# Products of half chunks dealt evenly to four array parts, one bank fewer per gate, masks first, and v's load first, in a one-core kernel of linear attention and a gated FFN

## The chip, the core and the metric

The kernel runs on one core of one Trainium2 chip. Its engines work side by side: TensorE (PE, matmuls; its weight loads are shown as PEld), VectorE (DVE), ScalarE (ACT), GpSimd (POOL) and SyncE (SP, which here only starts transfers). PE writes into PSUM, eight banks of 128 partitions by 2 KB, which DVE and ACT read; everything else lies in SBUF. The metric is the time of one execution in microseconds (us), as the median of several runs.

## The reference

The first half is gated linear attention for 4 batches of 8 heads, 768 steps, 48 values a head; the second is a multiplicative feed-forward network over the 3072 rows that this gives:

```
for t in range(S):                              # per batch b and head h
    state = alpha[t][:, None] * state + outer(k[t], v[t])     # 48 x 48
    y[t]  = q[t] @ state
x = y as 3072 rows of 384 (8 heads x 48)
out = (((x @ w1) * (x @ w2)) @ w3) @ w_out      # 384 -> 1024 -> 1024 -> 384
```

q, k, v and alpha are float32; the four weights come as float64.

## The kernel before

**Attention by chunks.** The 768 steps of a batch are cut into six chunks of C = 128, so there are N = 24 chunks, and the loop over n (L729 to L829) takes one chunk per step with all eight heads at once. For a chunk, `logs` and `decays` make the running products e of alpha (and their inverses) from a sum of logarithms; `decayed` (L357) multiplies q and k by them on DVE into qk; `transposed` turns qk on PE, 64 rows at a time, into qkT, whose two copies out of PSUM ACT makes (L383). `scores` forms all products of k and q in a chunk, and DVE clears what lies in the future with the masks of L440 and L457, which gives ms ("masks" below). A chunk's output y is then the sum of two products in PSUM: `attend_state` (L463), the state T of before the chunk times q, and `attend` (L477), v times ms. `outer` (L393) makes the next state from k and v, and at some chunks `advance` (L405) multiplies it on POOL with decays that have come back from DRAM. At each step n the order is: state and y's first part of chunk n-1, scores of chunk n, transposes of chunk n+1, `advance` and `turn_v`, the rest of y of chunk n-1, outer product of chunk n; in between, pieces of other work are dealt out (below).

**The array's parts.** Heads are worked on in pairs: the head pair j (0 to 3) has its two heads (i = 0, 1) in the partitions 0 to 47 and 64 to 111. A matmul that contracts over at most 64 partitions and writes at most 64 partitions occupies one of four parts of PE's array, given by the half of the rows that it reads from (i) and the half of the partitions that it writes; matmuls on different parts run at the same time. From chunk TURNED = 8 on, `turned_scores` (L422) leaves out the scores that the masks would clear: a chunk is cut into two halves of 64 steps, and the scores of the later half's keys are made for the later half's queries only. So of each head the part that takes the earlier keys streams 128 columns, the other 64. What is left out of the masks saves attention work as well: queries of the earlier half need v's earlier half only, and this product is `attend_low` (L415). It contracts over 64 steps, and for the second head of a pair over v with its halves exchanged, which `turn_v` (L162) makes by two copies on POOL into `vts`. `attend_low` of chunk n-1 is woven into the scores of chunk n, two matmuls behind each j:

```
if turned(n - 1):
    for i in range(2):
        attend_low(n - 1, j % 2, i, i ^ (j < 2))
```

The last argument is the half of the partitions that it writes: with j = 0 and 1 the part is (i, 1-i), with j = 2 and 3 it is (i, i). The longer scores of head i fall on part (i, i). After the last chunk, L755 to L757 issue these lows without scores.

**Where y lies.** y of a chunk has two banks, one for each row half i; in a bank, pair j lies in the upper or lower partitions and its 128 queries side by side. `attend_state` writes each with one matmul of 128 columns (8 for a chunk), the two kinds of v products add to it, and two copies on ACT (L489) bring it to SBUF, from where `store` sends it to the DRAM array xd.

**The gates and the rest.** A float32 product is made of parts rounded for PE: x and w are split in three (high, low, and a third that both corrections share), and `products` (L554) runs K/128 matmuls each for two of the parts into one group, and K/128 for the third. `exact` (L557) does this with two banks: ACT copies the first, scaled, to SBUF (L563), and DVE scales the second and adds it (L565). `onto` (L575) uses one bank: ACT scales it in place (L579), and the third part's matmuls are put off in a list `pending` until `settle` runs them on top. A gate tile is one 128-row piece of (x @ w1) * (x @ w2) for the columns of a group of three or four chunks; early gates, those made while attention runs, use `exact` for both factors, and DVE multiplies them (L602):

```
for factor, scale in zip(factors(g, f), (1.0, P * P)):
    r.append(gw.tile([C, width], FP32, tag="g", name="r"))
    exact(r[-1], *factor, scale)
```

Early gates wait in the list `fill`; `run(pieces)` takes one half tile (one factor, nine matmuls) per piece, at three places of a step, so that there are up to three in a step. The groups are begun by `begin` (L723): group g at chunk 3+4g, with `split_early` splitting its x at the step that is two later. Late gates use `onto` for both factors; behind attention they run with the folding of w3 @ w_out into one matrix w3o (`fold`), and then `project` multiplies chunk by chunk with it.

**The start.** Until step FIRST = 6 there are no gates; the steps then convert w1 and w2 from float64 (`convert`, pieces of `to_fp32`, L244 to L253) on ACT and DVE, beside the attention of the first chunks. `load_early(0)` reads x of the first three chunks back (L512).

**What sets the order.** Each engine runs its instructions in the order in which the program issues them, unless `after_marks` holds one back behind a marked instruction of another engine's list; a scheduler may set instructions that are held back behind later ones. In the loop of before, `decayed(n + 2)` is held behind the masks of chunk n only for n < 3. SyncE's queue takes loads and stores in the program's order: `store` (y), `load_a` (alpha), `load_kq`, then `load_v` (L154), which for chunks 3 to 7 goes by POOL's queue. The pool of PSUM has eight banks, dealt out in turn: a new bank is the one that was freed first, and the first matmul into it waits until it is read.

Of the kernel before, what the change touches and what calls it, by code (L numbers as in the profile page):

```python
# [10 lines left out]
FP32 = mybir.dt.float32  # L11
# [9 lines left out]
P = 4096.0  # L21
# [27 lines left out]
def kernel(  # L49
# [112 lines left out]
    def turn_v(n):  # L162
        if turned(n):
            for half in range(2):
                nc.gpsimd.tensor_copy(out=vts[n % 2][ds(DP * half, DP), :, 0:D],
                                      in_=st["v", n][ds(DP * (1 - half), DP), 1::2, 0:D])
# [248 lines left out]
    def attend_low(n, jj, i, half):  # L415

        s, w = ds(DP * i, DP), (vts[n % 2] if i else st["v", n])
        h = half * NP // 2 + jj
        nc.tensor.matmul(st["y", n][0][i][ds(DP * half, DP), jj, 0:DP], w[s, h if i else 2 * h, :],  # L419
                         st["ms", n][s, i, h, 0:DP], start=(n % NCH == 0 and jj == 0), stop=True, skip_group_check=True)  # L420

    def turned_scores(n):  # L422
# [3 lines left out]
        for j in range(NP):  # L426
# [5 lines left out]
            if turned(n - 1):  # L432
                for i in range(2):
                    attend_low(n - 1, j % 2, i, i ^ (j < 2))
# [30 lines left out]

# [11 lines left out]
    def attend(n):  # L477
        (y, heads), ms, vc = st.pop(("y", n)), st.pop(("ms", n)), st.pop(("v", n))
        for j, i, to in heads:
            if turned(n):  # L480
                w = vts[n % 2][:, j, :] if i else vc[:, 2 * j, :]
                nc.tensor.matmul(to[:, DP:], w, ms[:, i, j, DP:], start=False,  # L482
                                 stop=(j % HP == HP - 1), skip_group_check=True)
            else:
                nc.tensor.matmul(to, vc[:, 2 * j + i, :], ms[:, i, j, :], start=(n % NCH == 0 and j % HP == 0),  # L485
                                 stop=(j % HP == HP - 1), skip_group_check=True)
        x = work.tile([C, HP, 2, C], FP32, tag="x", name="x", bufs=4)
        for i in range(2):
            copied = nc.scalar.copy(x[:, :, i], y[i])  # L489
        ends_of_part1[1] = copied.ins  # L490
        x = x.rearrange("p j i t -> p (j i) t")

        to = xd.rearrange("(b h d) t -> b d h t", b=2, d=D)
# [63 lines left out]
    def exact(to, w, x, scale, in_place=True):  # L557
# [5 lines left out]
        nc.scalar.activation(t, p1, AF.Copy, scale=(1.0 + 1.0 / P) * scale)  # L563
        products(p2, w, x, (2,), n, True, True)
# [357 lines left out]
```

## Time and profile before

| | |
|---|---|
| median of 3 runs | 463.27 us (463.22 to 464.31) |
| the profiled execution | 462.59 us |
| its span, first to last instruction | 460.9 us |
| PE busy | 446.0 us (97%), 4080 matmuls |
| DVE busy | 370.6 us (80%) |
| ACT busy | 270.7 us (59%) |
| POOL busy | 87.4 us (19%) |
| granted TensorE clock | 0.999 |

The span falls into three stretches, whose busy times are:

| stretch, us | what runs | PE | DVE | ACT |
|---|---|---|---|---|
| 0 to 57 | start: loads, conversion of w1 and w2, chunks 0 to 6 | 47.95 | 41.70 | 39.48 |
| 57 to 187 | attention, chunks 6 to 23, with early gates | 127.78 | 117.81 | 82.20 |
| 187 to 457 | late gates, w3 @ w_out, projection | 270.00 | 210.53 | 149.05 |

A busy time is the time in which at least one instruction of the engine ran, in an execution recorded by the hardware profiler. Matmuls overlap, and their ends are modelled, so what a group of them costs is read from one first start to the next group's first start. "bank" is the name of every PSUM tile, and "L554" the line of the kernel that issued an instruction.

### The profile page before, as it was taken

To read this page: it belongs to the slowest core of one execution; us is meant where nothing else is said; L and a number is where in the kernel's file an instruction comes from. 1 tells how busy PE (TensorE), PEld (TensorE's weight loads), DVE (VectorE), ACT (ScalarE), POOL (GpSimd) and SP (SyncE) were. 2 spreads that over 40 slices of the span, in tenths; PEclk is the share of its full clock that TensorE was granted. 3 is DMA by queue.
4 is the path that set the end of the run, shared out by engine and by line. 5 is a ranking of instruction groups with operands and counts; after the bars stand their busy time and mean duration, and the time that the engine had idled before them with its cause. 6 is when DMAs were issued, how large, how long until landed. Compare 5 with 4: busy or idle time off the path is not lost.

```text
span 460.9 us, 10654 instructions
## 1 busy us (share of the span) xinstructions
PE 446.0 (97%) x4080; PEld 394.6 (86%) x4080; DVE 370.6 (80%) x600; ACT 270.7 (59%) x507; POOL 87.4 (19%) x171
## 2 busy tenths in 40 slices
PE   4998999899999999999999999999999999999996
PEld 2676699898989988888888888888888999999996
DVE  2897997999979989798999899999537566776671
ACT  4685966667668563787975757566436333343430
POOL 6134332324414370012021010100000000000000
PEclk9999999999999999999999999999999999999999
DMA  9999999989999965436966364521119655665511
GB/s 174 258 215 226 263 216 208 233 208 226 188 225 186 254 153 167 138 102 187 302 193 207 118 172 133 175 70 46 48 51 288 197 151 165 188 186 158 160 53 51
DMA packets 149379, 79.95 MB, mean 173 GB/s; under 512 B 97184, under 2 KB 138784, under 8 KB 149328
## 3 DMA queue, kind: packets, MB, share of 16 engines
q1 hardware_dynamic: 143840, 64.84, 57.0%
q0 software_dynamic: 5488, 14.43, 10.5%
q8 instruction: 32, 0.52, 0.5%
q14 instruction: 19, 0.16, 0.1%
HBM read 57.19 MB, written 22.06 MB: 172 GB/s over the span
## 4 chain that ended last, share of the span: by engine, by line
PE 89%; DVE 6%; issue 2%; ACT 2%; DMA 1%; DVEq 0%; ACTq 0%
PE bank L554 73%; PE bank L381 3%; PE bank L430 3%; PE bank L482 2%; PE bank L474 2%; DVE qk L359 1%; PE bank L393 1%; PE bank L340 1%; PE bank L346 1%; DVE ms L457 1%; PE bank L454 1%; PE bank L343 1%; PE bank L419 1%; PE bank L485 1%; DMA ac<-in_alpha_dram 1%
## 5 line engine op out<-in xcount | busy, mean ns | idle before, releaser
L554 PE MATMUL bank<-x,w 128*128 128x512 f32 (+1 forms) x688 | 162.7, 374 | 1.5 <-ACT qkT L383 1.2
L554 PEld LDWEIGHTS bank<-x,w 128*128 128x128 f32 x688 | 124.8, 188 | 21.3 <-ACT qkT L383 1.5
L554 PE MATMUL bank<-w3o,ab 128*128 128x384 f32 x576 | 100.2, 336 | 0.0
L554 PEld LDWEIGHTS bank<-w3o,ab 128*128 128x128 f32 x576 | 99.9, 188 | 0.2
L554 PE MATMUL bank<-x3b,w 128*128 128x512 f32 (+1 forms) x248 | 71.9, 385 | 0.0
L579 ACT ACTIVATE bank<-bank 128x512 f32<-128x512 f32 (+1 forms) x72 | 41.0, 571 | 33.1 <-PE bank L554 33.1
L554 PEld LDWEIGHTS bank<-x3b,w 128*128 128x128 f32 x248 | 46.4, 188 | 8.3
L628 POOL DMA_DIRECT2D abd<-r x33 | 19.3, 584 | 138.1 <-DVE r L614 116.2
L678 DVE TENSOR_TENSOR ab<-abl,ab 128x1024 fp32r<-128x1024 f32 x24 | 29.4, 1224 | 14.2 <-ACT ab L677 14.2
L383 ACT COPY qkT<-bank 128x512 f32<-128x512 f32 x48 | 26.1, 599 | 23.1 <-PE bank L381 23.1
L563 ACT ACTIVATE t<-bank 128x384 f32<-128x384 f32 x24 | 11.8, 493 | 45.9 <-PE bank L554 45.9
L677 ACT ACTIVATE ab<-abl 128x1024 fp32r<-128x1024 f32 x24 | 25.5, 1062 | 21.8 <-PE bank L554 19.8
L554 PE MATMUL bank<-wo,w3T 128*128 128x384 f32 x192 | 36.3, 337 | 0.0
L554 PEld LDWEIGHTS bank<-wo,w3T 128*128 128x128 f32 x192 | 34.1, 188 | 1.2
L565 DVE SCALAR_TENSOR_TENSOR o<-bank,t 128x384 f32<-128x384 f32 x24 | 13.4, 558 | 26.1 <-issue 14.3
L249 ACT ACTIVATE power<-power,rebias 128x512 uint32<-128x512 uint32 (+1 forms) x36 | 25.2, 701 | 15.0 <-DVE power L248 14.7
L359 DVE TENSOR_TENSOR qk<-kq,e 128x768 f32<-128x768 f32 x24 | 23.2, 965 | 10.5 <-ACT e L350 7.7
L565 DVE SCALAR_TENSOR_TENSOR r<-bank,r 128x384 f32<-128x384 f32 (+1 forms) x40 | 22.9, 578 | 8.5 <-ACT r L563 5.0
L563 ACT ACTIVATE r<-bank 128x384 f32<-128x384 f32 (+1 forms) x40 | 20.8, 524 | 14.7 <-PE bank L554 12.5
L614 DVE TENSOR_TENSOR r<-bank,r 128x512 f32<-128x512 f32 x32 | 21.9, 684 | 9.2 <-PE bank L554 7.7
L679 DVE SCALAR_TENSOR_TENSOR ab<-ab,abl 128x1024 fp32r<-128x1024 f32 x24 | 29.2, 1218 | 0.0
L251 DVE SCALAR_TENSOR_TENSOR mant<-mant,raw 128x512 f32<-128x512 uint32 (+1 forms) x36 | 23.5, 652 | 2.6 <-ACT raw L244 2.6
(115 smaller groups left out, 741.7 us busy)
## 6 DMA issues: line engine op xcount, KB each, us to landing
abl<-abd SPq DMA_DIRECT2D x24, 512.0 KB, 4.2
abd<-r POOLq DMA_DIRECT2D x33, 256.0 KB, 3.5
raw<-in_moe_w_dram SPq DMA_DIRECT2D x64, 128.0 KB, 3.7
raw<-in_moe_w_dram SPq DMA_DIRECT2D x12, 512.0 KB, 5.9
kq<-in_k_dram SPq DMA_DIRECT2D x24, 192.0 KB, 5.0
kq<-in_q_dram SPq DMA_DIRECT2D x24, 192.0 KB, 5.4
xd<-x SPq DMA_DIRECT2D x48, 96.0 KB, 3.7
xT<-xd POOLq DMA_DIRECT2D x6, 768.0 KB, 5.3
```

The lines of the kernel that those rows point to most:

```text
L249: nc.scalar.activation(power, power, AF.Relu, scale=2.0 ** 23, bias=rebias)
L251: nc.vector.scalar_tensor_tensor(mant, top, 2.0 ** -20, rest, op0=ALU.mult, op1=ALU.add)
L359: mark["qk", n] = nc.vector.tensor_mul(qks[n % 3][:, :, :, 0:D], st.pop(("kq", n)), st.pop(("e", n)).rearrange("p i (h d) -> p i h d", h=H ...
L383: mark["qkT", n] = nc.scalar.copy(qkT[:, :, :, ds(DP * half, DP)], tp[half]).ins
L554: nc.tensor.matmul(p, w[part][i], x[part][i], start=start and part == parts[0] and i == 0, stop=stop and part == parts[-1] and i == n - 1, ...
L563: nc.scalar.activation(t, p1, AF.Copy, scale=(1.0 + 1.0 / P) * scale)
L565: nc.vector.scalar_tensor_tensor(to, p2, scale, t, op0=ALU.mult, op1=ALU.add)
L579: nc.scalar.activation(p, p, AF.Copy, scale=1.0 + 1.0 / P)
L614: nc.vector.tensor_mul(r[0], p, r[0])
L677: nc.scalar.activation(t[:, 0], ab, AF.Copy, scale=1.0 - 2.0 ** -13)
L678: nc.vector.tensor_sub(t[:, 1], ab, t[:, 0].bitcast(FP32))
L679: nc.vector.scalar_tensor_tensor(t[:, 2], t[:, 0].bitcast(FP32), -1.0 - 1.0 / P, ab, op0=ALU.mult, op1=ALU.add)
```

## The change

It has five parts.

1. **Products dealt evenly.** y of a turned chunk is laid out anew: one bank holds the queries of the later half of a chunk, y[0], the other those of the earlier half, y[1], for all four pairs j. `attend_low` now always writes the half 1-i of the partitions, so that all lows fall on the parts (0, 1) and (1, 0), which take the shorter scores. `attend_state` cuts each product with the state into two of 64 columns, one for each half of the queries, and deals them to all four parts: 16 matmuls of 64 columns in place of 8 of 128. Both row halves i now write into one bank, in opposite halves of its partitions; before, each bank had one row half only. `attend` copies y[1] first, by two copies of 64 partitions each, because its heads lie exchanged, then makes the later half's products into y[0] and copies it whole. y is stored by head instead of by half of the heads.
2. **The second factor of an early gate** is made by `onto`: ACT scales the bank in place, the last three matmuls of nine are put off, and DVE multiplies the bank with the first factor directly. `exact` gets a hook `between`, where the pending matmuls of the tile before are run, behind the first six matmuls of the next first factor; a `settle()` behind `outer` runs them too. The last tile of a group (`begin_last`) keeps `exact` for both factors. The scale P * P goes to the first factor.
3. **Masks first.** `decayed(n + 2)` is held behind the masks of chunk n for n <= 6 instead of n < 3.
4. **v's load first.** From step 6 on `load_v(n + 2)` stands first in the step, ahead of stores and of the loads of alpha, k and q; before step 6 it stands behind `advance` instead of ahead of the conversion.
5. **v's turning earlier.** `turn_v(n + 1)` runs near the end of step n, where `turn_v(n)` ran in step n; `advance(n)` is held behind it.

```
-    def attend_low(n, jj, i, half):
-        s, w = ds(DP * i, DP), (vts[n % 2] if i else st["v", n])
-        h = half * NP // 2 + jj
-        nc.tensor.matmul(st["y", n][0][i][ds(DP * half, DP), jj, 0:DP], w[s, h if i else 2 * h, :],
-                         st["ms", n][s, i, h, 0:DP], start=(n % NCH == 0 and jj == 0), stop=True, skip_group_check=True)
+    def attend_low(n, j, i):
+        s, w = ds(DP * i, DP), (vts[n % 2][:, j, :] if i else st["v", n][:, 2 * j, :])
+        nc.tensor.matmul(st["y", n][1][ds(DP * (1 - i), DP), j, :], w[s], st["ms", n][s, i, j, 0:DP],
+                         start=(n % NCH == 0 and j == 0), stop=(j == NP - 1), skip_group_check=True)
...
     def attend_state(n):
         qkT = st.pop(("qkT", n))
+        if turned(n):
+            y = st["y", n] = [bank()[:, 0:NP * DP].rearrange("p (j c) -> p j c", c=DP) for _ in range(2)]
+            if n % NCH:
+                for j in range(NP):
+                    for t in range(2):
+                        for i in range(2):
+                            r = ds(DP * i, D)
+                            nc.tensor.matmul(y[t][ds(DP * (i ^ t), DP), j, :], Ts[n % 2][r, j, :],
+                                             qkT[r, 1, j, ds(DP * (1 - t), DP)],
+                                             start=(j == 0), stop=False, skip_group_check=True)
+            return
...
     def attend(n):
...
+        if turned(n):
+            x = work.tile([C, NP, C], FP32, tag="x", name="x", bufs=4)
+            for i in range(2):
+                nc.scalar.copy(x[ds(DP * i, DP), :, 0:DP], y[1][ds(DP * (1 - i), DP)])
+            for j in range(NP):
+                for i in range(2):
+                    nc.tensor.matmul(y[0][ds(DP * i, DP), j, :], vts[n % 2][:, j, :] if i else vc[:, 2 * j, :], ms[:, i, j, DP:],
+                                     start=(n % NCH == 0 and j == 0), stop=(j == NP - 1), skip_group_check=True)
+            copied = nc.scalar.copy(x[:, :, DP:], y[0])
...
-    def exact(to, w, x, scale, in_place=True):
+    def exact(to, w, x, scale, in_place=True, between=lambda: None):
...
         nc.scalar.activation(t, p1, AF.Copy, scale=(1.0 + 1.0 / P) * scale)
+        between()
         products(p2, w, x, (2,), n, True, True)
...
     def early_gate(g, f):
-        r, width = [], st["x3", g][2]
-        for factor, scale in zip(factors(g, f), (1.0, P * P)):
-            r.append(gw.tile([C, width], FP32, tag="g", name="r"))
-            exact(r[-1], *factor, scale)
-            if len(r) == 1:
-                yield
-        nc.vector.tensor_mul(r[0], *r)
-        store_ab()
-        st["ab"] = g, f, r[0]
+        first, second = factors(g, f)
+        width, closing = st["x3", g][2], f == begin_last[g]
+        r = gw.tile([C, width], FP32, tag="g", name="r")
+        exact(r, *first, P * P, between=settle)
+        yield
+
+        def done(p):
+            nc.vector.tensor_mul(r, p, r)
+            store_ab()
+            st["ab"] = g, f, r
+
+        if closing:
+            t = gw.tile([C, width], FP32, tag="g", name="r")
+            exact(t, *second, 1.0)
+            done(t)
+        else:
+            onto(*second, width, done, 1)
...
     for n in range(N + 1):
+        if n >= FIRST:
+            load_v(n + 2)
...
-        if n >= FIRST:
-            load_v(n + 2)
...
-                    attend_low(n - 1, j % 2, i, i ^ (j < 2))
+                    attend_low(n - 1, j, i)
...
-        if n < FIRST:
-            with after_marks("pool"):
-                load_v(n + 2)
...
-        advance(n)
-        turn_v(n)
+        with after_marks(*[("vt", n)] * turned(n)):
+            advance(n)
+        if n < FIRST:
+            with after_marks("pool"):
+                load_v(n + 2)
         if n:
             attend(n - 1)
         outer(n)
+        settle()
...
-        with after_marks(*[("ms", n)] * (n < 3)):
+        with after_marks(*[("ms", n)] * (n <= FIRST)):
             decayed(n + 2)
...
+        turn_v(n + 1)
         run(pieces > 2)
```

More of the change, by code (lines that the diff above doesn't have):

```diff
@@ L164, in turn_v @@
             for half in range(2):
-                nc.gpsimd.tensor_copy(out=vts[n % 2][ds(DP * half, DP), :, 0:D],
-                                      in_=st["v", n][ds(DP * (1 - half), DP), 1::2, 0:D])
+                mark["vt", n] = nc.gpsimd.tensor_copy(out=vts[n % 2][ds(DP * half, DP), :, 0:D],
+                                      in_=st["v", n][ds(DP * (1 - half), DP), 1::2, 0:D]).ins
     XA, XB = 2 * KM * 4 * C, KM * 4 * C
@@ L477, in attend @@
     def attend(n):
[L478 to L482, printed above, removed]
-                                 stop=(j % HP == HP - 1), skip_group_check=True)
[L484 to L489, printed above, removed]
+        y, ms, vc = st.pop(("y", n)), st.pop(("ms", n)), st.pop(("v", n))
+        to = xd.rearrange("(h i d) t -> i d h t", i=2, d=D) if turned(n) else xd.rearrange("(b h d) t -> b d h t", b=2, d=D)
+        if turned(n):
[8 more added lines that the diff above has]
+        else:
+            y, heads = y
+            for j, i, o in heads:
+                nc.tensor.matmul(o, vc[:, 2 * j + i, :], ms[:, i, j, :], start=(n % NCH == 0 and j % HP == 0),
+                                 stop=(j % HP == HP - 1), skip_group_check=True)
+            x = work.tile([C, HP, 2, C], FP32, tag="x", name="x", bufs=4)
+            for i in range(2):
+                copied = nc.scalar.copy(x[:, :, i], y[i])
+            x = x.rearrange("p j i t -> p (j i) t")
         ends_of_part1[1] = copied.ins
-        x = x.rearrange("p j i t -> p (j i) t")
-        to = xd.rearrange("(b h d) t -> b d h t", b=2, d=D)
         for half in range(2):
@@ L595, in early_gate @@
     def early_gate(g, f):
-        r, width = [], st["x3", g][2]
-        for factor, scale in zip(factors(g, f), (1.0, P * P)):
-            r.append(gw.tile([C, width], FP32, tag="g", name="r"))
-            exact(r[-1], *factor, scale)
-            if len(r) == 1:
-                yield
-        nc.vector.tensor_mul(r[0], *r)
-        store_ab()
-        st["ab"] = g, f, r[0]
+        first, second = factors(g, f)
[11 more added lines that the diff above has]
+            done(t)
+        else:
+            onto(*second, width, done, 1)
     def late_gate(g, f):
@@ L724 @@
     loads = {8: 1, 11: 2, 15: 3, 20: 4}
+    begin_last = {g: tiles[-1] for g, tiles in begin.values()}
     def early_pair(n):
@@ L756 @@
                 for i in range(2):
-                    attend_low(n - 1, j % 2, i, i ^ (j < 2))
+                    attend_low(n - 1, j, i)
         transposed(n + 1)
```

## The prediction

> **What bounds the kernel now.** I read the page first (span, busy time, slices, chain), then what TensorE (PE) waited for, then the timeline of PE inside one turned step, then VectorE (DVE), ScalarE (ACT) and SyncE's queue where PE is not yet full.
>
> ```profile
> span 460.9 us, 10654 instructions
> PE 446.0 (97%) x4080; PEld 394.6 (86%) x4080; DVE 370.6 (80%) x600; ACT 270.7 (59%) x507; POOL 87.4 (19%) x171
> PE   4998999899999999999999999999999999999996
> DVE  2897997999979989798999899999537566776671
> PE 89%; DVE 6%; issue 2%; ACT 2%; DMA 1%; DVEq 0%; ACTq 0%
> ```
>
> PE is full in nearly every slice and carries 89% of the chain. DVE is nearly as full up to slice 28, so an edit that only relieves DVE is worth nothing unless PE waits for it. From 57 to 190 us PE's own waits are these three, and no DMA is among them:
>
> ```profile
> PE bank L554 <- ACT qkT L383: 1.2, 1, 1.2
> PE bank L381 <- issue: 0.7, 1, 0.7
> PE bank L554 <- DVE r L565: 0.2, 1, 0.2
> ```
>
> So behind 57 us time is won only by shorter matmul stretches or by those 2 us. The timeline of PE (start, length, engine, line, records; an fp32 matmul is two records) first shows the step whose scores stand alone, then one with scores and the lower halves of attention together, then the last step's lower halves alone:
>
> ```profile
> 67.46 1.05 PE L430 MATMUL bank<-qkT 48*64 48x128 f32 x32
> 68.44 0.71 PE L381 MATMUL bank<-ident,qk 64*128 64x64 f32 x16
> ...
> 98.39 0.67 PE L474 MATMUL bank<-qkT,T 48*64 48x128 f32 x16
> 98.88 0.38 PE L430 MATMUL bank<-qkT 48*64 48x128 f32 x7
> ...
> 99.09 0.40 PE L430 MATMUL bank<-qkT 48*64 48x128 f32 x8
> ...
> 99.31 0.40 PE L430 MATMUL bank<-qkT 48*64 48x128 f32 x8
> ...
> 99.65 0.40 PE L430 MATMUL bank<-qkT 48*64 48x128 f32 x6
> ...
> 100.09 0.28 PE L381 MATMUL bank<-ident,qk 64*128 64x64 f32 x2
> ...
> 186.15 0.22 PE L419 MATMUL bank<-ms,v 64*64 64x64 f32 x2
> 186.20 0.22 PE L419 MATMUL bank<-ms,v 64*64 64x64 f32 x2
> ```
>
> Starts matter here, not lengths, since records overlap. With j=0 and 1 the lows fall on the two array parts that the scores use less: 0.21 and 0.22 us per j. With j=2 and 3 they fall on the two that the scores use more: 0.34 and 0.44 (the last holds the passage to the transposes). Before 57 us the bound is DVE, and behind it loads:
>
> ```profile
> 36.68 0.69 DVE L253 TENSOR_TENSOR mant<-mant,power 128x512 f32<-128x512 f32 x1
> 39.95 0.96 DVE L359 TENSOR_TENSOR qk<-kq,e 128x768 f32<-128x768 f32 x1 [2.58 <-ACT raw L244]
> 40.83 1.28 DVE L457 TENSOR_TENSOR ms<-bank,keep 128x512 int32<-128x512 int32 x2
> ...
> 48.41 0.37 SPq L512 DMA_DIRECT2D x3b<-xd  x1
> ...
> 53.90 1.23 ACT L521 ACTIVATE x<-x3b 128x1152 fp32r<-128x1152 f32 x1
> ...
> 57.00 3.32 PE bank L554 x18
> ```
>
> DVE idles 2.58 us with chunk 4's masks queued behind a qk whose load had not landed; the scores they need ended at 37.2.
>
> **The change, part by part.** (1) Scores with lows, 15 steps (chunks 8 to 22). All lows now go to the two lighter parts, so each of the four parts streams the same. The stretch is 1.21 us (98.88 to 100.09); scores alone, whose fullest part then streams as much as each part will, take 0.98 (67.46 to 68.44), and 0.21+0.22+0.22+0.33 from the j's gives 0.98 as well. I take 0.23 us. Two of the 15 stand ahead of a wait that DVE and ACT set (4), where PE only waits longer: 13 x 0.23 = -3.0 (bounds: 15 x 0.25 and 13 x 0.17).
>
> (2) State products: 8 matmuls of 128 columns become 16 of 64, in 14 chunks (two begin a batch). Now 98.39 to 98.88, 0.49 us. The nearest row for four parts at 64 columns is the last step's lows: a group of four records each 0.05 to 0.06 us. Eight such rounds and a first start of 0.06 are 0.52: +0.03 x 13 = +0.4. Lower bound 0; upper 32 records at 0.018 (16 records, 186.03 to 186.32) = 0.58, +1.3. The TensorE page of the Trainium skill ("TensorE: Matmul & The Clock Gate", section "Wait — 56ns, not 53.3ns?") states that matmul starts never come closer than about 25 ns; here 16 started in 0.24 us, 15 ns each, so the trace disagrees for matmuls on different parts.
>
> (3) The last step's lows stand alone and now use two parts of four: 8 rounds of 0.055 and the passage are 0.6 against 0.39 (186.03 to 186.42): +0.2.
>
> (4) Banks. The low half of y has a bank of its own, copied by two half-height ACT copies that stand ahead of qkT's. One more copy per chunk; pairs of such copies start 0.26 us apart, so 16 x 0.26 = 4.2 us on ACT, which is 55 to 75% busy there: free while ACT waits for the transposes (19.1 us in 12 waits between 57 and 187), else up to 0.26 per short step, four of them, +1.0. The bank is free sooner. At 85.69 PE waited 1.19 us for a bank that qkT's copy held, behind an ACT instruction waiting for DVE. In the built order the three matmuls that waited now use the early-freed bank, the next six wait for the same copy: 3 x 0.173 = -0.5 (bounds 0 and -1.2). The wait at 167.97 was for a bank held by y's copy behind four ACT instructions of the last split; now the transposes take earlier banks: -1.0, of which 0.5 comes back as PE reaches the last split's products before DVE has made them: -0.5.
>
> (5) Gates. 16 combining instructions leave DVE (its list is 16 shorter), 16 x 578 ns = 9.2 us. PE does the same matmuls and waited 0.2 us for them: 0. The cover is PE's own queue; if it were gone, DVE would still be the freer engine. What is added: one bank held over a step, with its last three matmuls after ACT's in-place scaling; attention's matmuls stand between, so ACT is long done.
>
> (6) Masks ahead of qk for chunks 3 to 6 (the order changes for 4, 5 and 6). Chunk 4's masks move from 40.83 to 37.4. Behind them the weight's step, power and so ACT's queue come about 3 us sooner, and with them transposes 6 (44.93). qk, now queued behind the masks, loses little: its load sets it. But L512 was issued at 48.41 behind stores and loads that SP issues without a gap, takes 5.1 us to land, and ACT began at 53.90 as soon as it was there. PE would be ready at about 54.9 instead of 56.93, then wait for DVE's L522 (1.36 us, to about 56.1) and L524 (to about 57.5): its first 15 matmuls end near 58.7 instead of 59.7. I take -1.0; ends +0.3 and -3.0.
>
> (7) v's load passes two stores, alpha's and kq's two loads on SP's queue, which go one issue (0.4 to 1.5 us) later; PE and DVE show no wait for them behind 57 us. Up to chunk 7 it goes behind `advance` on POOL's queue, whose last step then starts up to 0.9 us sooner. `turn_v`'s two copies move a step earlier and `advance` waits for them, so its state product waits for v's landing; readers of T come 4 us later. 0, with 0.5 either way.
>
> Sum: -3.0 +0.4 +0.2 -0.5 -0.5 -1.0 = -4.4 us. The profiled execution took 462.59 us (span 460.9 and 1.7 around it) and would take 458.2; the median of 463.27 is 0.7 above it, so I forecast 458.9.
>
> **Rivals.**
> - Smaller: the start's lead dies at L512's load and ACT's extra copies keep the two waits: -3.0 +0.4 +0.2 = -2.4, 460.9. For it: the load's landing. Chance 0.20, a quarter of it within 0.3% of before.
> - Larger: the start's lead passes whole, -2.0 more: 456.9. For it: PE is continuous from 50.7 on; against it the same load. 0.11.
> - Slower, by one mechanism: two matmuls on different row halves of the array cannot write one bank together. Before, each row half had its own bank; now both write the same one, in opposite halves of its partitions. Then a state round's pair takes turns, half hidden behind the other bank's pair: +8 x 0.058 x 14 = +6.4; the lows' pairs cost +0.2 per step instead of -0.23, +3.0; the last step +0.6; with -2.0 of (4) and (6), +8.0: 471.3. It decides from about a third of that price, 20 ns a round. No row of before has such a pair, so the trace speaks neither way; for my sum only that the two write different partitions. 0.12. "TensorEngine Tiling (Array Packing)" of the Trainium skill states this rule ("Gotcha 1: PSUM Pressure"); no row shows it.
> - Slower, a floor on starts: the eight score records of a j start 0.21 us apart, 27 ns each. Could none start closer, 32 records would take 0.86 (+0.37 x 14 = +5.2), scores with lows would gain nothing, and with -1.8 of (3), (4) and (6) it is 466.7. The 15 ns of (2) speak against it. 0.02.
> - A bank held by a pending product, or y's copies ahead of qkT's, makes PE wait some 0.4 us in most of 16 steps: 463 to 465. Against it: DVE gains room. 0.12, half of it within 0.3%.
>
> **How the numbers follow.** My own sum has 0.43. About 0.3% is what a measurement here can tell from no change (461.9 to 464.7). Faster: 0.43 + 0.15 + 0.11 = 0.69; same 0.05 + 0.06 = 0.11; slower 0.06 + 0.12 + 0.02 = 0.20. The first three cases hold 0.74; with (1), (2) and (6) at their ends they run from 456.4 to 462.3. To leave out no more than 2 in 10 the range takes in the nearer half of the last rival, to 464.0; my own case alone runs from 457.9 to 459.9, half-way to its neighbours.
>
> **What would show it.** Scores with lows near 0.98 us from first start to the transposes, state products near 0.52, the last step's lows near 0.6; no PE wait over 1 us at the last split; L554 first before 56 us with gaps in its first nine; L565 on r 16 fewer. Wrong if the state products reach 0.8 or more, or if PE waits for DVE or ACT in turned steps.

## The result, and the profile after

The changed kernel takes 465.93 us (median of 8 runs, 464.57 to 467.56) against 463.00 (8 runs): a ratio of 1.0071, with a 95% interval of 1.0055 to 1.0086. It is slower by 0.7%; the forecast was 458.9 us in a range of 456.4 to 464.0. The profiled execution took 466.79 us. All eight executions of the changed kernel show a granted clock of 0.993 to 0.996; those of the kernel before, in each session below, fall for the most part in two groups, with 0.998 or more and with 0.993 or less, and the median of the second lies 0.2 to 1.5 us higher.

The page of the changed kernel: span, busy times, the granted clock in 40 slices, and the chain.

```profile
span 465.1 us, 11106 instructions
PE 446.9 (96%) x4304; PEld 395.4 (85%) x4304; DVE 362.3 (78%) x584; ACT 278.6 (60%) x523; POOL 84.1 (18%) x172
PEclk9999979999999999999999999999999999999999
PE 80%; DMA 8%; DVE 4%; issue 3%; ACT 2%; POOL 1%; SPq 1%; POOLq 0%; DVEq 0%; ACTq 0%
```

PE is as busy as before (446.9 for 446.0 us), but one slice shows a lower clock, and DMA now has 8% of the chain for 1%. What PE waited for from 57 to 190 us:

```profile
PE bank L566 <- ACT bank L592: 3.4, 2, 3.0
PE bank L566 <- ACT qkT L383: 0.6, 1, 0.6
PE bank L471 <- issue: 0.4, 1, 0.4
PE bank L566 <- DVE r L578: 0.4, 1, 0.4
```

The place of the 3.0 us, in the timelines of SyncE's queue, ACT and PE (start, length, what; in brackets the idle time before it and its releaser):

```profile
52.64 0.40 SPq L157 DMA_DIRECT2D v<-in_v_dram  x1
53.13 1.75 SPq L305 DMA_DIRECT2D xd<-x  x2
54.97 0.43 SPq L151 DMA_DIRECT2D kq<-in_k_dram  x1
55.46 2.18 SPq L152 DMA_DIRECT2D kq<-in_q_dram  x1
57.73 0.93 SPq L145 DMA_DIRECT2D ac<-in_alpha_dram  x1
...
61.00 0.49 ACT L575 ACTIVATE r<-bank 128x384 f32<-128x384 f32 x1
63.85 0.52 ACT L324 ACTIVATE la<-ac 128x384 f32<-128x384 f32 x1 [2.36 <-DMA ac<-in_alpha_dram]
64.28 0.47 ACT L592 ACTIVATE bank<-bank 128x384 f32<-128x384 f32 x1
...
61.12 0.67 PE L393 MATMUL bank<-v,qk 128*64 128x48 f32 x16
64.80 1.01 PE L566 MATMUL bank<-x,w 128*128 128x384 f32 x2 [3.01 <-ACT bank L592]
```

Alpha of chunk 11 is issued at 57.73 us (54.41 before) and lands at 63.83 (59.59 before). Its logarithm L324 stands on ACT ahead of L592, the new scaling of a gate's bank in place, and the gate's put-off matmuls wait for L592. Before, the same logarithm started at 60.53 and held nothing up:

```profile
54.41 2.12 SPq L145 DMA_DIRECT2D ac<-in_alpha_dram  x1
...
60.53 0.65 ACT L324 ACTIVATE la<-ac 128x384 f32<-128x384 f32 x1
```

Four windows of the changed kernel's stretch (length, then busy time and count of PE, PEld, DVE, ACT and POOL, then the granted clock, the DMA engines' busy share and GB/s) show what follows:

```profile
60.22:63.63 3.41, 1.51 (x32) 1.14 (x28) 3.41 (x7) 1.27 (x3) 1.21 (x3) 1.00 0.98 151
63.63:67.05 3.42, 2.25 (x7) 2.25 (x8) 1.71 (x4) 1.98 (x5) 0.51 (x1) 0.50 0.81 283
67.05:70.46 3.41, 3.41 (x13) 3.41 (x12) 1.44 (x3) 0.49 (x1) 0.00 (x0) 0.50 0.97 224
70.46:73.87 3.41, 3.41 (x45) 3.16 (x45) 1.90 (x3) 2.07 (x5) 1.38 (x3) 1.00 0.88 201
```

PE is idle for 1.9 of the first 3.41 us, and for the next 6.8 us its clock is half. The start of each chunk's transposes (first L381 record) is a ruler for the whole:

| transposes of chunk | before, us | changed, us | difference |
|---|---|---|---|
| 8 | 56.33 | 55.12 | -1.21 |
| 9 | 68.44 | 74.62 | +6.18 |
| 12 | 91.60 | 96.93 | +5.33 |
| 17 | 128.82 | 132.32 | +3.50 |
| 21 | 156.95 | 160.25 | +3.30 |
| 23 | 167.51 | 171.65 | +4.14 |
| end of the span | 460.89 | 465.08 | +4.19 |

One step, between chunk 8 and chunk 9, loses 7.4 us. The steps to chunk 21 win 2.9 back, the last two lose 0.8, and the late stage is the same. The loss of that step is explained in what follows as one chain, theory A of the expectations below: a late alpha, its logarithm ahead of L592 on ACT, PE without a bank to go on with, and a halved clock behind PE's wait. The stretches of PE that the prediction priced, here one turned step of the changed kernel:

```profile
102.90 0.69 PE L471 MATMUL bank<-qkT,T 48*64 48x64 f32 x32
103.41 0.39 PE L429 MATMUL bank<-qkT 48*64 48x128 f32 x8
...
103.64 0.39 PE L429 MATMUL bank<-qkT 48*64 48x128 f32 x8
...
103.85 0.39 PE L429 MATMUL bank<-qkT 48*64 48x128 f32 x8
...
104.07 0.27 PE L429 MATMUL bank<-qkT 48*64 48x128 f32 x1
...
104.46 0.71 PE L381 MATMUL bank<-ident,qk 64*128 64x64 f32 x16
```

The j's now start 0.23, 0.21 and 0.22 us apart. From first start to the next group's first start (medians), scores with lows take 1.045 us for 1.219 (but 1.10 to 1.37 in the four steps that have no gate pieces, the "short steps" below), the state products 0.515 for 0.488, the last lows alone 0.564 for 0.391.

### The profile page after: what moved, and what is told of

Its sections match the earlier page's. It is cut to its first block, busy times and chain, and to the rows that moved or that the text cites. A ratio compares the mean times of both kernels' runs of the same rounds, so it can differ in the third digit from the quotient of the medians.

```text
span 465.1 us, 11106 instructions
## 1 busy us (share of the span) xinstructions
PE 446.9 (96%) x4304; PEld 395.4 (85%) x4304; DVE 362.3 (78%) x584; ACT 278.6 (60%) x523; POOL 84.1 (18%) x172
## 4 chain that ended last, share of the span: by engine, by line
PE 80%; DMA 8%; DVE 4%; issue 3%; ACT 2%; POOL 1%; SPq 1%; POOLq 0%; DVEq 0%; ACTq 0%
PE bank L566 69%; DMA ac<-in_alpha_dram 3%; DMA dec<-ends 2%; DMA ends<-e 2%; PE bank L429 2%; PE bank L381 2%; PE bank L471 1%; PE bank L493 1%; PE bank L346 1%; PE bank L343 1%; DMA raw<-in_moe_w_out_dram 1%; PE bank L418 1%; PE bank L393 1%; DVE x3b L536 1%; SPq L236 1%
## 5 line engine op out<-in xcount | busy, mean ns | idle before, releaser
L566 PE MATMUL bank<-x,w 128*128 128x512 f32 (+1 forms) x688 | 165.8, 378 | 4.2 <-ACT bank L592 3.0
L566 PEld LDWEIGHTS bank<-x,w 128*128 128x128 f32 x688 | 127.0, 191 | 24.1 <-ACT bank L592 3.1
L592 ACT ACTIVATE bank<-bank 128x512 f32<-128x512 f32 (+1 forms) x88 | 49.2, 560 | 38.4 <-PE bank L566 38.3
L575 ACT ACTIVATE t<-bank 128x384 f32<-128x384 f32 x24 | 11.9, 495 | 45.9 <-PE bank L566 45.9
L383 ACT COPY qkT<-bank 128x512 f32<-128x512 f32 x48 | 25.8, 588 | 7.5 <-PE bank L381 7.2
L635 DVE TENSOR_TENSOR r<-bank,r 128x512 f32<-128x512 f32 x32 | 21.8, 683 | 9.5 <-PE bank L566 8.5
L252 DVE SCALAR_TENSOR_TENSOR power<-raw,power 128x512 uint32<-128x512 uint32 (+1 forms) x36 | 23.9, 664 | 0.4 <-ACT power L249 0.4
L253 DVE TENSOR_TENSOR mant<-mant,power 128x512 f32<-128x512 f32 (+1 forms) x36 | 23.8, 660 | 0.3
```

The costliest lines, as they stand in the source:

```text
L252: nc.vector.scalar_tensor_tensor(power, high, 0x80000000, power, op0=ALU.bitwise_and, op1=ALU.bitwise_or)
L253: nc.vector.tensor_mul(mant, mant, power.bitcast(FP32))
L383: mark["qkT", n] = nc.scalar.copy(qkT[:, :, :, ds(DP * half, DP)], tp[half]).ins
L566: nc.tensor.matmul(p, w[part][i], x[part][i], start=start and part == parts[0] and i == 0, stop=stop and part == parts[-1] and i == n - 1, ...
L592: nc.scalar.activation(p, p, AF.Copy, scale=1.0 + 1.0 / P)
L635: nc.vector.tensor_mul(r[0], p, r[0])
```

## The experiments

Kernels that ran together share their runs of the kernel before; its median was 463.4 to 464.4 us. Single executions of it lie 2 us below to 4 us above that, so a time is read with its interval, and the cause from the trace. Each kernel has one trace.

**Taking the chain of the lost step apart.** v's load back behind alpha, k and q from step 6 on:

```
-        if n >= FIRST:
-            load_v(n + 2)
         if not 1 < n < FIRST:
...
+        if n >= FIRST:
+            load_v(n + 2)
         late_state = early_pair(n - 1)
```

> The changed kernel, with v's load from step 6 on put back behind the loads of alpha, k and q. Theory A (one chain: v's load ahead of alpha's on SyncE's queue makes alpha of chunk 11 land at 63.8 us instead of 59.6; its log stands on ACT ahead of the in-place scaling that the first gate's put-off matmuls wait for; PE idles 3.0 us and its clock falls to 0.5 for some 6.8 us): alpha lands before 62, that wait is under 0.5 us, the clock stays at 1.00, and the time falls by 5 to 7 us, to about 460. Theory B (the start's new order had already delayed the queue, x's load being issued 1.4 us later before v passes anything): the wait stays over 2 us and the time within 1.5 us of the changed kernel's 465.9.

466.12 us, ratio 1.0059 (1.0036 to 1.0081): not faster. Alpha was issued at 55.50 and landed at 62.16, and ACT was held for 0.58 us instead of 2.36, with a PE wait of 0.36; that part of A holds. B is right in the time, though not about the wait that it named: the start had already put alpha 1.1 us back, and in this run PE waited 2.2 us from 54 us on for y's copies, which stood on ACT behind the split of x, itself waiting for its load. The clock was half from 56.5 on, behind that wait. The lead of the start had run into x's load. A later alpha then held ACT for 2.84 us, and PE waited 1.8 us for L592 from 117.6 on.

The one logarithm out of the way:

```
-        nc.scalar.activation(p, p, AF.Copy, scale=1.0 + 1.0 / P)
+        mark["on"] = nc.scalar.activation(p, p, AF.Copy, scale=1.0 + 1.0 / P).ins
...
-            with after_marks(*[("qkT", n + 1)] * (n < N - 4)):
+            with after_marks(*[("qkT", n + 1)] * (n < N - 4), *["on"] * (n == FIRST + 1)):
                 logs(n + 4)
```

> The changed kernel, with the log of chunk 11 held behind the in-place scaling of the first gate on ACT; every load stays where the change put it. Theory A: PE doesn't wait for alpha any more although it lands as late as 63.8; no wait over 0.5 us between 57 and 75, clock 1.00, about 460. Theory B' (late loads cost PE time in other ways too, through qk or v): the wait moves to a transposition or to the outer product, at least half of the 3.0 us stays, 463 or more.

464.98 us, ratio 1.0011 (0.9984 to 1.0039). Alpha landed even later, at 64.26, and PE did not wait for it: no wait over 0.14 us at the first gate, the transposes of chunk 9 at 69.42 instead of 74.62. So the hold is what made the 3.0 us. It came back at the next late alpha: at 89.24 ACT had been held 2.36 us, PE waited 2.2 us for L592, and the clock was half from 92.69 on.

Both factors in two banks again:

```
     def early_gate(g, f):
-        first, second = factors(g, f)
...
+        r, width = [], st["x3", g][2]
+        for factor, scale in zip(factors(g, f), (1.0, P * P)):
+            r.append(gw.tile([C, width], FP32, tag="g", name="r"))
+            exact(r[-1], *factor, scale)
...
         outer(n)
-        settle()
```

> The changed kernel, with both factors of an early gate made in two banks each as before (nothing put off). Theory A: alpha still lands near 63.8 and its log still holds ACT, but the gate's third parts go into a bank of their own, so PE goes on: the wait falls under 1.5 us and the clock stays at 1.00; 460 to 461.5. Rival C (late alpha is enough: with ACT held, the banks run out in any form of the gate): a wait of 2 us or more at the same place, the clock falls, 464 or more.

464.20 us, ratio 1.0011 (0.9984 to 1.0038). ACT was held by alpha nearly as long as in the changed kernel (1.93 us, to 62.75), yet PE waited 0.17 us there and the clock stayed at 1.00: A, not C. A late alpha costs this much only together with a bank that is scaled in place: with the old gates, the longest wait of PE for a gate's copy behind such a hold was 0.7 us (in the run with masks first alone). Nor does every hold cost something with the new gates: in the run with the gates alone ACT was held 1.85 us, to 116.54, and PE did not wait.

**The parts alone.** The even dealing on the kernel before (`attend_low`, `attend_state` and `attend` as in the change):

```
-                    attend_low(n - 1, j % 2, i, i ^ (j < 2))
+                    attend_low(n - 1, j, i)
```

> The kernel before, with the even dealing alone (lows, state products, y's layout and copies). From the stretches of the changed kernel: 15 scores with lows at 1.045 us for 1.219 (-2.6), 13 state products at 0.515 for 0.488 (+0.35), the last lows 0.564 for 0.391 (+0.17): -2.1 us, 461 against 463. Rival: the third ACT copy of y makes PE wait in the short steps, 0.3 us or more in half of them, and the time is 463 or more.

468.84 us, ratio 1.0100 (1.0065 to 1.0135): slower. The ten steps with gates, chunk 9 to 23, became shorter (80.8 us for 83.9 in all), but the four steps without gates (chunks 10 to 11, 14 to 15, 18 to 19, 22 to 23) took 21.4 us for 15.2. In them PE waited 0.8 us for masks and 2.2 us for v's exchanged halves (L165 on POOL, 168.58 to 170.81), with a halved clock behind each. What the change does with v takes away a wait that the dealing brings.

Masks first, alone:

```
-        with after_marks(*[("ms", n)] * (n < 3)):
+        with after_marks(*[("ms", n)] * (n <= FIRST)):
             decayed(n + 2)
```

> The kernel before, with the masks first up to the seventh step, alone. By the prediction's step 6: the transposition of chunk 6 about 1 to 2 us sooner than before (44.9), the first gate's matmuls near 56.5, the time -1.0 us (462.0 to 462.5). Rival (the lead only meets the loads: x of the first gate and the next k and q land no sooner): the transposition of chunk 9 at 68.4 us or later as before, and the time within 0.5 us of before; above 464 if PE idles 2 us or more at x's load and its clock falls.

465.17 us, ratio 1.0046 (1.0024 to 1.0068). The transposes of chunk 6 came at 43.68 for 44.93, the first gate at 55.76 for 56.93, those of chunk 9 at 67.90 for 68.44: the lead is there and shrinks. But from chunk 9 to 23 the same instructions took 101.3 us for 99.1. ACT was held by alpha three times (0.59, 1.52 and 3.32 us) for once before (2.15). PE's waits from 57 to 190 us add up to 4.2 us for 2.2. An earlier PE meets loads that are no earlier.

The gates alone:

```
+        exact(r, *first, P * P, between=settle)
...
+            onto(*second, width, done, 1)
```

> The kernel before, with the second factor of the early gates in its bank, alone. By the prediction's step 5: nothing, within 0.7 us of before. Rival, from the changed kernel's short steps, which are as long as before's while those with the old gates are 0.9 to 1.3 us longer: the relief of DVE is worth something only where PE has less to do, so alone it is worth 0 to -0.5 us. Theory C (in-place scaling makes PE wait for ACT by itself): waits of 1 us or more for it and 464.5 or more.

464.85 us, ratio 1.0032 (1.0011 to 1.0052): between the cases, for the time is theory C's, but PE waited only 0.7 us for the in-place scaling. Its start, which is that of before, had a halved clock from 44.06 to 50.88. Of the rival's 0 to -0.5 us nothing is to be seen, and what made this kernel slower isn't shown.

v's load first from step 6 on, alone:

```
+        if n >= FIRST:
+            load_v(n + 2)
         if not 1 < n < FIRST:
             store()
```

> The kernel before, with v's load first from step 6 on, alone. Prediction's step 7: 0, within 0.5 us of before. Theory A for the old gates: alpha of chunk 11 lands near 61 to 62 in place of 59.6 and holds ACT for 0.5 to 1 us, no gate waits for a scaling in place, but ACT's copies get late: +0 to +1.5 us.

462.57 us, ratio 0.9973 (0.9948 to 0.9998): the one kernel of all that was faster than before, by an interval that nearly reaches no change. Its ACT around the first gate:

```profile
61.40 0.58 ACT L563 ACTIVATE r<-bank 128x384 f32<-128x384 f32 x1
63.64 0.52 ACT L324 ACTIVATE la<-ac 128x384 f32<-128x384 f32 x1 [1.66 <-DMA ac<-in_alpha_dram]
64.07 0.47 ACT L563 ACTIVATE r<-bank 128x384 f32<-128x384 f32 x1
```

The same late alpha holds ACT for 1.66 us, and PE doesn't wait: the second factor has a bank of its own.

**Other orders of the loads.** Alpha first, then v:

```
         if n >= FIRST:
+            load_a(n + 5)
             load_v(n + 2)
```

> The changed kernel, with alpha's load put ahead of v's from step 6 on; v still stands ahead of stores, k and q. Theory A (alpha late on the queue, its log ahead of the in-place scaling on ACT): alpha of chunk 11 is issued near 53 us and lands before 59, so ACT is never held by a log for more than 0.5 us, PE's waits for the in-place scaling (3.4 us in the changed kernel) go below 0.7, the clock stays at 1.00 from there on, and the time falls from 465.9 to 459.5 to 461.5. Rival (DMA is simply too full there: v or k and q become late instead): PE's waits between 54 and 100 us stay at 2.5 us or more, for qk, v's copies or T, and the time is 463 or more.

467.26 us, ratio 1.0082 (1.0055 to 1.0110). ACT was never held by a logarithm, as A has it, and the transposes of chunk 9 came at 68.35. But the time went the rival's way, though through another load: the store of a gate's product, issued at 100.02 us, landed at 106.68, and the chain sets the next gate's copy L575 (106.76) behind it. PE waited 1.2 us for that copy and 1.0 us for the masks right behind it, and the clock was half from 111.9 to 115.4. The four short steps took 20.7 us.

The start and step 6 as before:

```
-        if n >= FIRST:
+        if n > FIRST:
             load_v(n + 2)
...
+        if n == FIRST:
+            load_v(n + 2)
...
-        with after_marks(*[("ms", n)] * (n <= FIRST)):
+        with after_marks(*[("ms", n)] * (n < 3)):
```

> The changed kernel, with the order of the start and of step 6 put back (the masks first up to chunk 2 only, v's load as before up to step 6; v first from step 7 on). Theory A: alpha of chunk 11 lands near 59.6 as before, nothing holds the first gate; the transposition of chunk 9 is at 68.4 to 69 us as before, and behind it the step times of the changed kernel stay (-2 us in all): 460.5 to 462. If the short steps' waits or the one-bank gates cost by themselves: 463 or more.

464.30 us, ratio 1.0021 (0.9995 to 1.0047). The lost step was 12.15 us, as before (12.11), and from chunk 9 to 23 it took 97.9. In this run the start had a wait of 2.2 us for chunk 4's masks and a halved clock from 45.3 to 52.1, so that chunk 9 began at 70.88 all the same. This is the wait that "masks first" takes away; in the profiled run of before it was 0.85 us. In the eight traces with the old start PE waits 0.6 to 3.8 us for these masks, with the clock half behind it in five; in the twelve with masks first it never waits for them. But in nine of those twelve it then waits 0.7 to 2.2 us near 55 us for y's copies, behind the split of x.

The dealing with v's earlier turning and first load from step 7 on, without the gates and the start (against the changed kernel):

```
-        exact(r, *first, P * P, between=settle)
+            exact(r[-1], *factor, scale)
...
-        with after_marks(*[("ms", n)] * (n <= FIRST)):
+        with after_marks(*[("ms", n)] * (n < 3)):
```

> The even dealing with v's earlier turning and v's load first from step 7 on, without the new gates and with the old start. If the old gates' DVE work is what takes the dealing's gain back in the short steps: those four steps are 0.9 us longer each or more than before (3.97, 4.14, 3.69, 3.42), the gated steps 0.2 to 0.4 shorter, and the time is 463.5 to 465; without that give-back 461 to 462.

463.97 us, ratio 0.9998 (0.9964 to 1.0033). The wait for v's halves is gone. Gated steps 81.2 us for 83.9, short steps 18.5 for 15.2: the give-back is there, but not at 0.9 us each. Two of the four bear it (+2.18 and +1.02), and their waits (2.05 us in the lows L418, 0.86 in the scores L429) have no releaser; the profile names no wait for masks in them. So DVE's relief is not what this run shows.

**What a wait costs.** Five pauses in the projection, where PE is full:

```
+            z = lastp.tile([C, DM], FP32R, tag="z", name="z", bufs=1)
+            nc.gpsimd.tensor_copy(out=z, in_=t)
+            for _ in range(2 - 1):
+                nc.gpsimd.tensor_copy(out=z, in_=z.bitcast(FP32))
+            products(p2, w, x, (2,), KF, True, True)
+            nc.tensor.matmul(pz, z[:, 0:C], z, start=True, stop=True)
```

> The kernel before, with five pauses of PE put into the last stage, where it is full: in the projection of chunks 4, 8, 12, 16 and 20 one more matmul waits for a chain of two copies on POOL. The chain is worked out to end 0.5 to 1.5 us behind PE. Each pause should cost its own length and 0.17 us for the matmul, and the clock should stay at 1.00: +3 to +8 us.

> The same with five copies on POOL, so that each pause is some 3 us longer than in the last. Theory (a wait of PE of over about 2 us also halves the clock for 3.4 us or more behind it): each pause costs its length and 1.7 to 3.4 us more, and the granted clock shows 0.5 behind each. Rival (the halved clock in the changed kernel has another cause): each costs its own length, the clock stays at 1.00.

PE's waits in the last stage, first with two copies on POOL, then with five; and windows of the second:

```profile
PE bank L698 <- POOL z L696: 2.0, 5, 0.4
```

```profile
PE bank L698 <- POOL z L696: 14.9, 5, 3.0
```

```profile
377.90:381.54 3.64, 0.65 (x5) 0.64 (x5) 3.01 (x3) 1.06 (x1) 2.76 (x4) 1.00 0.65 198
381.54:384.95 3.41, 3.41 (x12) 3.41 (x12) 0.38 (x1) 0.00 (x0) 0.00 (x0) 0.50 0.47 137
384.95:388.37 3.42, 3.42 (x21) 3.42 (x21) 0.68 (x2) 1.55 (x2) 0.00 (x0) 1.00 0.07 22
```

Short: 468.44 us (ratio 1.0111, 1.0090 to 1.0132), pauses of 0.4 us, no halved clock behind any. Long: 489.20 us (1.0567, 1.0534 to 1.0600), pauses of 2.98 us, and the clock is half behind four of five, for 3.41 us three times and 6.83 once. By the medians, +25.8 us is 5 x (2.98 + 0.17) = 15.8 and 2.0 more per pause. In the profiled execution the stage from the transposes of chunk 23 on took 316.6 us for 293.4, so 7.5 us more than 15.8; half of the 17.1 us at half clock is 8.5. The theory holds for four pauses of five; the other one fell across two windows of the clock's grid (see the last section), with 1.57 and 1.41 us idle in them. Of the short one, 5.0 us for 2.9 counted, the same stage took 3.2 us more; the other part lies ahead of it, where PE waited 3.8 us for chunk 4's masks and the clock was half from 44.4 to 51.2, which the pauses can't cause. One of its four executions kept a clock of 1.00 and still took 467.56, so the excess isn't settled.

**Repairs.** Calls of the logarithms at the end of each step, without and with v's old place:

```
-        if not early:
+        if n == FIRST:
             with after_marks(*[("qkT", n + 1)] * (n < N - 4)):
                 logs(n + 4)
...
         run(pieces > 2)
+        if n > FIRST:
+            with after_marks(*[("qkT", n + 1)] * (n < N - 4)):
+                logs(n + 4)
```

> The changed kernel, with the log of each step from the seventh on made at the end of its step, behind all gate pieces; loads as in the change. Theory A, widened by what the run with one log held back showed (whenever alpha lands late, its log holds ACT and with it the gate copies that PE needs; put off at one place, it happens at the next, at 89 us): with no log ahead of a gate copy, PE has no wait over 1 us between 57 and 170 us, the clock stays at 1.00, the stretch from the transposition of chunk 9 to that of chunk 23 is 97 us or less (99.07 before, 97.03 in the changed kernel), and the time is 461 to 463. Rival (the loads themselves are the wall, alpha only the first of them): the waits move to qk, v or the gates' stores, and the time stays at 464 or more.

> As the last, with v's load behind alpha, k and q as before. Theory A: alpha lands sooner, and nothing else gets later but v: the same 461 to 463, at most 0.7 us away. Rival (loads are the wall): v's exchange of halves on POOL becomes late in the short steps, waits for it of 1 us or more, 464 or more.

465.41 us (1.0035, 1.0011 to 1.0059) and 465.23 us (1.0036, 1.0012 to 1.0059). The edit failed at its first aim: the scheduler still set the logarithm of chunk 11 ahead of L592, and PE waited 2.5 and 2.1 us there. So both say little on the rival.

With every logarithm held behind its step's last gate copy, and the same with v's load as before up to step 6:

```
-        nc.scalar.activation(p, p, AF.Copy, scale=1.0 + 1.0 / P)
+        mark["on"] = nc.scalar.activation(p, p, AF.Copy, scale=1.0 + 1.0 / P).ins
...
-        if not early:
+        if n == FIRST:
...
+        if n > FIRST:
+            with after_marks(*[("qkT", n + 1)] * (n < N - 4), "on"):
+                logs(n + 4)
```

> The changed kernel, with every log from the seventh step on held behind the last gate copy of its step on ACT (the run before this only moved the calls, and the log of chunk 11 still stood ahead of the first in-place scaling). Theory A: no hold of ACT by an alpha reaches a gate copy; the step from the transposition of chunk 8 to that of chunk 9 is 15 us or less (12.1 before, 19.5 in the changed kernel), no PE wait over 1.5 us behind 57 us, 461.5 to 463.5. Rival (the loads are the wall): 464.5 or more, with waits for T, qk, v or the gates' stores.

> The same, with v's load as before up to step 6 (masks first and the rest as in the change). Theory A: alpha of chunk 11 and x of the first gate land sooner by 0.5 to 1.5 us, and with them the first gate: 461 to 463, at or below the kernel before. Rival: as the last, 464.5 or more.

The first: 463.62 us, ratio 0.9985 (0.9956 to 1.0015), for 1.0071 of the change: the loss is gone, as A has it (14.26 us for the lost step, no PE wait of 0.15 us or more for L592 between 57 and 190 us). One PE wait of 1.6 us, which A did not expect, is taken up below; the clock was half for 3.4 us behind it. The second: 464.85 us, 1.0023 (0.9994 to 1.0053), against A: in its trace the first gate was well (12.94), but short steps took 21.8 us, with waits of 1.84 us in the lows and 1.2 for a gate's copy L575. ACT and PE's waits of the first:

```profile
60.00 0.49 ACT L575 ACTIVATE r<-bank 128x384 f32<-128x384 f32 x1
60.38 0.49 ACT L592 ACTIVATE bank<-bank 128x384 f32<-128x384 f32 x1
...
66.14 0.52 ACT L324 ACTIVATE la<-ac 128x384 f32<-128x384 f32 x1
```

```profile
PE bank L471 <- issue: 1.6, 1, 1.6
PE bank L418 <- issue: 0.5, 1, 0.5
PE bank L346 <- DVE la L329: 0.2, 1, 0.2
```

**The waits without a releaser.** The 1.6 us lie in the middle of the state products, between two groups that read the same tiles:

```profile
162.97 0.58 PE L471 MATMUL bank<-qkT,T 48*64 48x64 f32 x24
165.18 0.34 PE L471 MATMUL bank<-qkT,T 48*64 48x64 f32 x8 [1.63 <-issue]
```

The trace also has the packets of the instruction queue. The changed kernel fetches 34 pieces of 16 KB on it; PE has 4304 matmul and 4304 load records, so 8608 instructions fill 34 pieces at 256 each. In this run such a piece began at 161.7 us, took 2.08 and ended 1.39 us ahead of 165.18. To test it, tiny matmuls at the very start push the stream along:

```
+    pad = bank()
+    for _ in range(32):
+        nc.tensor.matmul(pad[0:DP - D, 0:DP - D], vts[0][:, 0, D:], vts[0][:, 0, D:], start=True, stop=True)
```

> The kernel with every log behind its step's gate copies, with 32 tiny matmuls (16 by 16, on zeros) more at the very start, where PE waits for its first load; their results are not used. In all traces so far PE's waits without a releaser in the profile (up to 2.1 us, in the lows of chunk 10 near 81 us and in the state products of chunk 22 near 168 us) end 1.25 to 1.55 us behind the last byte of a 16 KB piece of PE's own instruction stream. Theory F (they are waits for instructions, at the borders of the stream's pieces): 32 fp32 matmuls are 128 instructions, half a piece, so the borders fall elsewhere: no such wait over 0.3 us in these two groups; if the new places are less dense, the time falls by 0.5 to 2 us, to 462 to 463. Rival (a bank or an operand that the profile does not show): the waits stay in the lows of chunk 10 and the state products of chunk 22.

> The same with 64 tiny matmuls, 256 instructions or one whole piece. Theory F: the borders fall where they fell without them, and the waits without releaser are back in the lows of chunk 10 or the state products of chunk 22, each ending 1.25 to 1.55 us behind a fetch; the time within 1 us of 463.6. Rival: no difference between 32 and 64.

The waits after, with 32 (there the outer product is L397, the transposes L385) and with 64 (lows L422, state products L475):

```profile
PE bank L397 <- issue: 2.5, 1, 2.5
...
PE bank L385 <- issue: 0.3, 1, 0.3
```

```profile
PE bank L422 <- issue: 0.5, 1, 0.5
PE bank L475 <- issue: 0.4, 1, 0.4
```

Half a piece moves the waits out of the lows and the state products, to the outer product and the transposes; a whole piece brings them back, shorter. Theory F holds, as far as one trace of each goes. The hope of a gain doesn't: 466.24 us (1.0054, 1.0025 to 1.0082) and 465.01 (1.0017, 0.9994 to 1.0041). The new places were no less dense.

## Why the prediction was wrong

It failed at two of its steps together, and by a price that it didn't have. Its own sign of being wrong, a wait of PE for ACT in the turned steps, came true. Among ACT's waits from 57 to 187 us the trace of before already had one for alpha, which held nothing else up there:

```profile
ACT la L324 <- DMA ac<-in_alpha_dram: 2.1, 1, 2.1
```

- **Step 7, v's load, put at 0.** It said that alpha and kq go one issue later, and that PE and DVE show no wait for them. Alpha of chunk 11 was issued 3.3 us later: 1.6 because the queue came to that step later, 0.5 for v's issue, and 1.4 because the issue of q ahead of it took 2.18 us for 0.80. The one engine that reads alpha, ACT, was not looked at, nor what is queued behind its logarithm. Alone the step did no harm (0.9973).
- **Step 5, the gates, put at 0, with ACT "long done".** At the first gate ACT was held by that logarithm and PE waited 3.0 us. With the old gates the same hold cost PE 0.17 us. Neither step costs this alone; the prediction summed parts and had no term for two of them meeting.
- **No price for the clock.** A wait was counted at its length. Here 3.0 us of waiting and 6.8 us at half clock made most of the 7.4. Holding all logarithms back took the ratio from 1.0071 to 0.9985, some 4 us, and so showed the chain to be the loss against before.
- **Steps 1 to 3, the dealing.** Right in kind, too large in size: by the medians -0.174 us per step of scores with lows for -0.23. Summed over the 14 such stretches that transposes follow, it was 1.7 us, because in the short steps they took 1.10 to 1.37 us; why they did isn't known. +0.027 for +0.03 on the state products, +0.17 for +0.2 on the last lows. The rival that two row halves can't write one bank together falls: 32 records that write so took 0.515 us, not twice that. The rule in the Trainium skill's "TensorEngine Tiling (Array Packing)" ("Gotcha 1: PSUM Pressure") does not agree with this, as far as different partitions go; the measurement decides. The floor on starts falls with it: 32 records in 0.515 us are 16 ns each. (In the bank rival, 8 x 0.058 x 14 is 6.5 and not 6.4, which changes nothing.)
- **Step 4.** The wait at 85.69 went from 1.19 to 0.63 us, -0.56 for -0.5. The wait at 167.97 was put down to a held bank; it ends 1.44 us behind a piece of the instruction stream, like 29 others, and came back as 0.41 us in the state products.
- **Step 6, the masks, put at -1.0.** The lead of chunk 8 was 1.2 us and that of the first gate 0.28: its first matmul came at 56.65, not before 56. Alone the edit made the kernel slower (1.0046). The rival "smaller" had seen x's load as the end of the lead, but not that an earlier PE also meets later alphas.
- **That behind 57 us PE's work sets the time.** The changed kernel's steps from chunk 9 to 23 took 97.0 us for 99.1. Of the 14 kernels with the dealing, 11 gained 1.9 to 4.0 us in the gated steps, and all gave back 0.5 to 6.6 in the four short ones. PE at 97% hid that the loads landed just in time.

With the chain out of the way most of the forecast gain was still missing. In the trace of the first run with every logarithm held behind, the span is 0.6 us shorter than before: the start wins 2.4, the step to chunk 9 loses 2.2, the gated steps win 4.0, the short steps lose 3.2, and the late stage loses 0.4. What of the give-back is DVE, instruction stream or stores differs from run to run and isn't settled. No kernel with the even dealing was shown to be faster than before; v's load first alone (462.57 us) is the best of all, and one such interval among 18 kernels can be chance.

## What to carry to other kernels

Before moving a load on a full queue, ask which engine reads it first, what stands behind that instruction in its engine's order, and whether PE has any other bank to go on with; put just-in-time work like this logarithm behind what PE waits for, and read the built order to see that it is there. Price a wait of PE that takes 1.6 us or more of one 3.4 us window of the clock at more than its length (next section). Where short matmuls make an engine faster, count its instructions: the stream that feeds it comes by DMA, in pieces.

## What the runs showed of the hardware

**The clock has a grid of 3.413 us.** In each of the 20 traces the changes of the granted clock lie a multiple of 3.413 us apart; half clock inside a span lasted 3.413 or 6.827 us. The traces have 16 windows of this grid at full clock in which PE was idle for more than 1.6 us, and half clock followed all 16; below 0.94 us it followed none; in between it followed 8 and did not follow 23 others. In "TensorE: Matmul & The Clock Gate" (Part 1) the Trainium skill gives a free-running window of 3413 ns, which agrees; it also has the clock fall after at least one idle window, and here half of one was enough.

**PE waits for its own instructions.** All 30 waits of 0.25 us or more between 57 and 190 us to which the profiles give the name "issue", in 20 traces, end 1.23 to 1.81 us behind the last byte of a 16 KB piece on the instruction queue. The pieces of that stretch took 0.9 to 2.5 us, and the longest such wait was 2.5 us. A short step of the changed kernel holds 114 to 130 matmul records and as many loads, about a whole piece in some 4 us.
